# A low-rank tail of two products becomes a sixth chunk of a Strassen step, and the last products run by column slices

## The chip, the cores and the metric

The kernel runs on one core of a Trainium2 chip. Its time is the device time of one execution in microseconds (us). Each kernel is run several times on the same chip as the kernel it is compared with, and medians are compared. One execution is also recorded by the hardware profiler; its trace is what the views below come from.

The engines are called as in the profile: PE (TensorE matmuls; PEld is its weight loads), DVE (VectorE), ACT (ScalarE), POOL (GpSimd) and SP (SyncE, which only issues DMAs here). A name with a q behind it (SPq, ACTq) is an engine's sequencer.

## The reference

Two branches of the same input x (2048 tokens, 640 columns) are mixed by a gate for each token:

```python
a = x @ dft_hid_re.T                        # 640 x 640
b = x @ dft_hid_im.T
A = dft_seq_re @ a - dft_seq_im @ b         # 2048 x 2048 each
q = einsum("nd,dhc->nhc", x, w_q)           # 32 heads, 2 halves of 128
s1, s2 = q1 @ k1.T, q2 @ k2.T               # 16 scores each
...                                         # best 2 of each, best 2 of the 4 sums: 2 of 256 experts
act = gelu(<x, u[e]>);  B = sum over heads and choices of softmax(top)*act * v[e]
g = sigmoid((x * gate_w).sum(-1))
out = g * A + (1 - g) * B
```

## The kernel before

**Precision.** Every large product is made of three fp32r matmuls (`mm3`, lines 126 to 130): an operand is split into a high part, which ACT writes as a copy (line 123), and a low part, which POOL or DVE subtracts (line 124); the three are high × high, high × low and low × high. They show as lines L128, L129 and L130, and almost always have 512 columns.

**The pieces.** The sequence transform comes first, as it is the same work for both hidden matrices: 128 pieces (`seq_piece`; 2 matrices × 4 chunks of 512 tokens × 16 blocks of 128), each of 5 × 3 matmuls into 5 PSUM banks. NPC is their number. A chunk's result is copied out by ACT (L222), multiplied by the gate g on DVE (L193) and stored to DRAM. The other branch runs behind the pieces as a background program: a pump hands out its next step whenever PE has been given enough work. Its last stage builds for every token the weights of the 256 experts: DVE writes two sets of one-hot rows (`hot`, L634), PE multiplies them (L645), ACT masks the product (L604) and DVE sums it (`cd`, L610), after which it goes to DRAM (`gd`). The activations are in DRAM too (`actd`).

**The last part.** What is left is the transform over the hidden dimension, a product with inner length 2 × 640 for each of two halves of the tokens, and the expert branch's z × v, with z = weight × activation × (1 − g), 256 experts (2 rows of 128), and v 256 × 640. The stored chunks a11, a12, a21, a22 (two token chunks by two matrices) and the hidden matrices form a 2 × 2 block product, done by a Strassen form with seven unit products, `UNITS = ("a11", "a12", "s1", "s2", "s4", "s3", "a22")`, for 512 of the 640 columns (two groups of 128 times two). The last 128 columns are a plain product (role W) that rides along in four units. A unit goes over KD = 5 chunks of 128 inner rows; unit and chunk make a step, `step(m)`, 35 for each half (NSTEP), 70 in all. Sums of the token blocks (s1, s2, s3, s4) come from DRAM for the first half and from DVE for the second (`add_a`). Sums of the hidden matrices (`make_sums`, DVE, lines 731 to 735, then `split_sums`) are made among the last pieces.

Operands are split `AHEAD` = 5 steps early into a ring of six (`ring`): two slots of tile WP, four of WS. Raw operands lie in tiles `ra`, handed out by `take` and returned by `give`.

z comes in apart: `load_z` loads g, two rows of activations and two of weights (8 DMAs of 128 × 128); `split_z` makes z on DVE (lines 869 to 873) and splits it into `zo`; v is loaded by `load_v` (L749) at piece NPC − 3 and split at the last part's start (`split_v`); `z_group` adds z × v to the right accumulators at four places of a half.

**The order** is written out by hand: `at(n, f, ...)` has f issued after piece or step n, on whatever engines its instructions name; each engine then works through its instructions in the order of issue. The loads go on SP's queue.

**The end.** In the last unit of the second half the products of the second column group are held back until all others are issued; DVE then subtracts them in two pieces of 256 columns (L994), each followed by its DMA (L995), on SP's and ACT's queue.

Of the kernel before, what the change touches and what calls it, by code (L numbers as in the profile page):

```python
# [16 lines left out]
P = 128  # L17
S = 2048
D = 640
# [17 lines left out]
NSTEP = 7 * KD  # L37
# [54 lines left out]
def gated_mix_kernel(ctx: ExitStack, tc: tile.TileContext, xT, xn, dreT, dimT, wsre, wsim, wq, kT, uT, vv, gw, out):  # L92
# [624 lines left out]
    def t_sum(k, n, a):  # L717

        if n < 2:
            return TS[k][:, (2 * n + a) * 2 * P:][:, :2 * P]  # L720
        if n == 2:
            return TS[5 + k // 2][:, (2 * (k % 2) + a) * 2 * P:][:, :2 * P]
        return DD[:, 0, a, k, 2 * P:4 * P] if n == 3 else TS[k][:, PAIR + a * P:][:, :P]

    def make_sums(k):
        if k == 0:
            T["t"] = big.tile([P, 9 * P], F32, name="tf", tag="xl")
# [3 lines left out]
        nc.vector.tensor_sub(t[:, :4 * P].rearrange("p (n d) -> p n d", n=2), f[:, :, 0:2 * P], f[:, :, 2 * P:4 * P])  # L731
        nc.vector.scalar_tensor_tensor(t3, t1, -1.0, b22, op0=OP.mult, op1=OP.subtract)
        nc.vector.tensor_sub(t5, t1, t5)
        nc.vector.tensor_sub(t6, b22, b12)  # L734
        nc.vector.tensor_sub(t[:, 8 * P:], f[:, 1, 4 * P:], f[:, 0, 4 * P:])  # L735
        bg.credit -= 3.0

    def split_sums(k):
        for n in [k] + ([5 + k // 2] if k % 2 == 0 else []):
            TS[n] = big.tile([P, 2 * D], F32R, name="ts", tag=f"X{(1, 3, 4, 5, 6, 0, 2, 7)[n]}")  # L740
        t = T["t"]
        t1, t5, t3, t6 = (t[:, n * 2 * P:(n + 1) * 2 * P] for n in range(4))
        for n, f in enumerate((t1, t3, t5, t6, t[:, 8 * P:])):
            split(f, t_sum(k, n, 0), t_sum(k, n, 1), nc.gpsimd if n < 2 else nc.vector)
        bg.credit -= 1.0

    def load_v():
        T["f"] = big.tile([P, 2, D], F32, name="dt", tag="xf")
        nc.sync.dma_start(T["f"], vv.rearrange("k p d -> p k d"))  # L749

    def split_v():

        for t in ("xh", "xl"):
            T[t] = big.tile([P, 2, D], F32R, name="v" + t, tag=t)
        split(T["f"], T["xh"], T["xl"], nc.vector)
        for a, t in enumerate(("xh", "xl")):
            nc.scalar.activation(v_neg(a), T[t][:, :, 4 * P:], AF.Copy, scale=-1.0)

    def v_neg(a):
        return TS[5 + a][:, PAIR:].rearrange("p (k d) -> p k d", k=2)  # L760
# [5 lines left out]
    at(NPC - 3, load_v)  # L766
    at(NPC, split_v)
    at(NPC + 28, store_gates, 1)


    fresh, raw_free, raw_tags = deque(), deque(), [("wf", 1)] * 5 + [(f"X{s}", 2) for s in range(10, 16)] + [("xf", 2)]
    raw, sp = {}, {}

    def take(key):
        if not fresh and raw_tags:
            t, n = raw_tags.pop(0)
            if t == "wf":
                fresh.append(big.tile([P, TC], F32, name="ra", tag=t, bufs=5))
            else:
                r = big.tile([P, 2, TC], F32, name="ra", tag=t)  # L780
                fresh.extend(r[:, a] for a in range(2))
        raw[key] = f = (fresh or raw_free).popleft()
        return f
# [51 lines left out]
    def split_step(m):  # L835
        if m < 2 * NSTEP:
            b, (u, k) = m // NSTEP, divmod(m % NSTEP, KD)
            what = UNITS[u]
            key = (b, "s" if b and what in ("s1", "s2", "s4") else what, k)
# [3 lines left out]
            if b == 0 or what in ("a11", "a12", "a22", "s3", "s4"):  # L843
                give(key)

    zop = {}

    def load_z(b, n):
# [5 lines left out]
        for k in range(2):  # L854
            a, f = take((b, "za", k)), take((b, "zf", k))
            nc.sync.dma_start(a, actd[k][:, c * TC:(c + 1) * TC])
            for i in range(4):
                i8 = (4 * c + i) % 8
                nc.sync.dma_start(f[:, i * P:(i + 1) * P],
                                  gd[b][i8 // 4, i8 % 4].rearrange("e f m -> (e f) m")[k * P:(k + 1) * P])  # L860

    def split_z(b, n):

        if not zop:
            for k in range(2):
                zop[k] = big.tile([P, 2, TC], F32R, name="zo", tag=f"X{8 + k}")
        g = raw[b, "g", n]
        s = -1.0 if n == 0 else 1.0
        nc.vector.tensor_scalar(g, g, s, -s, op0=OP.mult, op1=OP.add)
        for k in range(2):  # L870
            a, f = raw[b, "za", k], raw[b, "zf", k]
            nc.vector.tensor_tensor(a, a, f, op=OP.mult)
            nc.vector.tensor_tensor(a, a, g, op=OP.mult)
            split(a, zop[k][:, 0], zop[k][:, 1], nc.gpsimd)
            give((b, "za", k))
            give((b, "zf", k))
        give((b, "g", n))
        bg.credit -= 3.5
# [19 lines left out]
    def post(b, what):  # L898
# [15 lines left out]
        elif what == "q":  # L914
            add("c22", "Y", OP.subtract)
# [5 lines left out]
    def z_group(o, c0, w, first=False, last=False, more=False):  # L921

        for k in range(2):
            h, l = zop[k][:, 0], zop[k][:, 1]
            for d in range(2):
                c = slice((c0 + d) * P, (c0 + d + 1) * P)
                mm3(roles[o][d], T["xh"][:, k, c], T["xl"][:, k, c], h, l, first and k == 0, last and k == 1, more)
                run_bg(0.68)
            if w:
                mm3(roles["W"], w(0)[:, k], w(1)[:, k], h, l, False, last and k == 1)  # L930
                run_bg(0.68)

    held = []

    def step(m):
        b, (u, k) = m // NSTEP, divmod(m % NSTEP, KD)
        what = UNITS[u]
        if k == 0:
# [8 lines left out]
            if what == "a22":  # L947
                z_group("Z", 0, v_neg, first=True)
        split_step(m + AHEAD)
        o, w, w5 = {  # L950
            "a11": ("X", lambda a: DD[:, 0, a, k, 0:2 * P], lambda a: DD[:, 0, a, k, 4 * P:]),
            "a12": ("Z", lambda a: DD[:, 1, a, k, 0:2 * P], lambda a: DD[:, 1, a, k, 4 * P:]),
            "s1": ("Y", lambda a: t_sum(k, 0, a), lambda a: DD[:, 0, a, k, 4 * P:]),
            "s2": ("X", lambda a: t_sum(k, 1, a), None),
            "s4": ("Y", lambda a: DD[:, 1, a, k, 2 * P:4 * P], None),
# [4 lines left out]
        end = k == KD - 1  # L960
        very_last = b == 1 and what == "a22"
        for d in range(1 if very_last else 2):
            c = slice(d * P, (d + 1) * P)
            mm3(roles[o][d], w(0)[:, c], w(1)[:, c], h, l, k == 0 and what in ("a11", "a12", "s1"),
                end and what not in ("a12", "s4"), more)
# [3 lines left out]
        if w5:  # L969
            mm3(roles["W"], w5(0), w5(1), h, l, k == 0 and what in ("a11", "s1"), end and what == "a22")  # L970
# [3 lines left out]
        if what == "a12":  # L974
            z_group("Z", 0, lambda a: T[("xh", "xl")[a]][:, :, 4 * P:], last=True)
        if what == "s4":
            z_group("Y", 2, None, last=True, more=True)
# [4 lines left out]
        if what == "s3":  # L982
            at(NPC + m, post, b, what)
            at(NPC + m, quarter, b)
        elif not very_last:
            at(NPC + m + 1, post, b, what)
        else:
            for d in range(2):
                if d == 1:
                    for n, x in enumerate(held):  # L990
                        mm3(roles["Z"][1], *x, False, n == KD - 1)
                for a in range(d + 1):
                    r = slice(a * TC // 2, (a + 1) * TC // 2) if d else slice(0, TC)
                    nc.vector.tensor_tensor(res["c"][:, d, r], res["c"][:, d, r], roles["Z"][d][:, r], op=OP.subtract)  # L994
                    (nc.scalar if a else nc.sync).dma_start(out[d][:, 3 * TC + r.start:3 * TC + r.stop],  # L995
                                                            res["c"][:, d, r])

    def quarter(b):
        roles["Y"] = [bank(3), bank(4)]
        z_group("Y", 2, None, first=True, last=True)  # L1000
        at(NPC + b * NSTEP + 6 * KD, post, b, "q")

    M = NPC
    for k in range(KD):
        at(M - 6 + k, load_a, 0, "a11", k, 1, 1)
        at(M - 4 + min(k, 3), load_a, 0, "a12", k, 1, 2)
        at(M + k // 2, load_a, 0, "s1", k, 0, 0)
        at(M + 2 + k, load_a, 0, "s2", k, 0, 0)
        at(M + 7 + k, load_a, 0, "s4", k, 0, 0)
        at(M + 12 + k, load_a, 0, "s3", k, 0, 0)  # L1010
        at(M + 18 + k, load_a, 0, "a22", k, 2, 2)
    M = NPC + NSTEP
    for k in range(KD):
        at(M - 8 + k, load_a, 1, "a11", k, 1, 1)
        at(M - 4 + k, load_a, 1, "a12", k, 1, 2)
        at(M + k, load_a, 1, "s", k, 2, 2)
        at(M + k, load_a, 1, "s3", k, 2, 1)
        at(M + 4 + k, add_a, 1, "s", "s3", k, False)
        at(M + 5 + k, load_a, 1, "a11", k, 1, 1)
        at(M + 8 + k, add_a, 1, "s", "a11", k, False)  # L1020
        at(M + 8 + k, add_a, 1, "s3", "a11", k, True)
        at(M + 8 + k, load_a, 1, "a12", k, 1, 2)
        at(M + 13 + k, add_a, 1, "s", "a12", k, True)
        at(M + 21 + k, load_a, 1, "a22", k, 2, 2)
# [79 lines left out]
```

## Time and profile before

| what | us |
|---|---|
| median of the 3 runs | 767.47 (766.01 to 768.31) |
| the profiled execution, its own time | 767.29 |
| its span in the trace | 765.5 |
| last part: from its first matmul to the span's end | 611.74 to 765.5 |
| PE busy, by the page | 759.2 |

The span is what the trace covers; 1.8 us of the profiled execution lie outside. In a row of a timeline the columns are start, duration, engine, line, operation, output and inputs by the program's names, and the number of instructions that were put together (x2), then in brackets the idle time ahead of it and what ended it. Matmul durations overlap, since they are pipelined; what counts is the distance of their starts. In a view of one line or tile the three durations are minimum, median and maximum in ns, with the first and the last start behind them.

### The profile page before, as it was taken

What the parts mean: (1) busy time and instruction counts of PE and PEld (TensorE: products, weight loads), DVE (VectorE), ACT (ScalarE), POOL (GpSimd) and SP (SyncE); (2) the same over time, 40 slices, a digit from 0 to 9 for tenths busy, and PEclk for the clock granted to TensorE, in tenths of its full rate; (3) what the DMA queues carried; (4) which work ended last, traced back from release to release, by engine and by line L of the source; (5) the groups of instructions that cost most, each with busy time, mean ns of one, the idle gap of its engine ahead of it and who ended that gap; (6) DMA issues with size and microseconds to landing.
All of it is one profiled execution on the core that took longest, in us unless ns stands there. A gap on an engine that the chain in (4) does not pass through costs nothing.

```text
span 765.5 us, 11060 instructions
## 1 busy us (share of the span) xinstructions
PE 759.2 (99%) x4085; PEld 620.5 (81%) x4085; DVE 554.9 (72%) x636; ACT 308.5 (40%) x548; POOL 335.1 (44%) x232
## 2 busy tenths in 40 slices
PE   9999999999999999999999999999999999999997
PEld 7777677888888888888888888888888788888886
DVE  6853151589899799999899899579978852437561
ACT  4434123321234432523532774533544653423350
POOL 5533235142242323423158674343456583549270
PEclk9999999999999999999999999999999999999999
DMA  9987996321212322310535352568874696766321
GB/s 336 354 310 187 354 383 204 110 75 42 76 55 75 112 97 62 124 51 21 167 127 167 117 157 73 176 183 272 279 237 166 209 325 212 247 192 196 123 84 69
DMA packets 75654, 130.33 MB, mean 170 GB/s; under 512 B 17104, under 2 KB 24400, under 8 KB 75344
## 3 DMA queue, kind: packets, MB, share of 16 engines
q1 hardware_dynamic: 63424, 113.23, 45.4%
q10 hardware_dynamic: 12176, 16.40, 6.0%
q8 instruction: 32, 0.52, 0.3%
q14 instruction: 22, 0.18, 0.1%
HBM read 102.84 MB, written 25.17 MB: 167 GB/s over the span
## 4 chain that ended last, share of the span: by engine, by line
PE 95%; DVE 2%; DMA 2%; ACT 1%; issue 0%; DVEq 0%
PE b L128 30%; PE b L129 30%; PE b L130 30%; PE b L333 2%; PE b L215 2%; DMA wq<-in_wq 1%; PE b L645 1%; DVE hot L634 1%; DMA wf<-in_wsre 0%; DVE ts L124 0%; DVE cd L610 0%; ACT b L604 0%; ACT ts L123 0%; DVE tf L731 0%; DVE tf L734 0%; DVE tf L735 0%
## 5 line engine op out<-in xcount | busy, mean ns | idle before, releaser
L124 POOL TENSOR_TENSOR WS<-wf,WS 128x512 fp32r<-128x512 f32 x127 | 194.1, 1531 | 257.6 <-ACT WS L123 239.9
L128 PE MATMUL b<-WS,X 128*128 128x512 f32 x620 | 243.4, 393 | 0.0
L129 PE MATMUL b<-WS,X 128*128 128x512 f32 x620 | 241.4, 389 | 0.0
L130 PE MATMUL b<-WS,X 128*128 128x512 f32 x620 | 241.3, 389 | 0.0
L128 PEld LDWEIGHTS b<-WS,X 128*128 128x128 f32 x620 | 116.4, 188 | 28.2 <-issue 3.6
L130 PEld LDWEIGHTS b<-WS,X 128*128 128x128 f32 x620 | 116.4, 188 | 24.3
L129 PEld LDWEIGHTS b<-WS,X 128*128 128x128 f32 x620 | 116.4, 188 | 23.6
L123 ACT ACTIVATE WS<-wf 128x512 fp32r<-128x512 f32 x127 | 79.7, 628 | 110.7 <-PE b L130 62.5
L634 DVE TENSOR_TENSOR hot<-rows,wtab 128x1024 f16<-128x1024 f16 x64 | 60.7, 972 | 15.7 <-PE b L645 15.7
L128 PE MATMUL b<-WU,xh 128*128 128x512 f32 x160 | 62.3, 390 | 0.0
L129 PE MATMUL b<-WU,xh 128*128 128x512 f32 x160 | 62.3, 390 | 0.0
L130 PE MATMUL b<-WU,xl 128*128 128x512 f32 x160 | 62.2, 389 | 0.0
L430 ACT ACTIVATE sc<-b 128x512 f32<-128x512 f32 x32 | 19.8, 618 | 104.6 <-PE b L130 104.6
L124 POOL TENSOR_TENSOR xl<-xf,xh 128x640 fp32r<-128x640 f32 x16 | 26.2, 1643 | 79.8 <-ACT xh L123 79.8
L124 POOL TENSOR_TENSOR WS<-ra,WS 128x512 fp32r<-128x512 f32 x32 | 44.3, 1407 | 27.0 <-ACT WS L123 26.8
L444 DVE TENSOR_REDUCE mm<-sc 128x64 f32<-128x1024 f32 x32 | 38.9, 1217 | 22.6 <-ACT sc L430 22.0
L604 ACT ACTIVATE b<-b,mask 128x128 f32<-128x128 f32 x128 | 43.3, 343 | 19.2 <-PE b L645 16.1
L446 DVE TENSOR_TENSOR eq<-sc,mm 128x1024 f16<-128x1024 f32 x32 | 48.6, 1519 | 1.1
L124 POOL TENSOR_TENSOR WP<-ra,WP 128x512 fp32r<-128x512 f32 x18 | 27.7, 1551 | 29.9 <-ACT WP L123 23.7
L450 DVE TENSOR_REDUCE rr<-eq 128x64 f16<-128x1024 f16 x32 | 39.0, 1220 | 1.1
L193 DVE SCALAR_TENSOR_TENSOR ST<-ST,grow 128x512 f32<-128x512 f32 x40 | 32.2, 863 | 10.1 <-ACT ST L222 10.1
L123 ACT ACTIVATE WS<-ra 128x512 fp32r<-128x512 f32 x46 | 28.3, 629 | 26.4 <-PE b L130 14.0
(155 smaller groups left out, 1217.7 us busy)
## 6 DMA issues: line engine op xcount, KB each, us to landing
wq<-in_wq SPq DMA_DIRECT2D x32, 640.0 KB, 7.6
wf<-in_wsim SPq DMA_DIRECT2D x64, 256.0 KB, 3.6
wf<-in_wsre SPq DMA_DIRECT2D x63, 256.0 KB, 4.7
ra<-pd SPq DMA_DIRECT2D x50, 256.0 KB, 3.8
pd<-ST ACTq DMA_DIRECT2D x35, 256.0 KB, 4.3
xf<-in_xT SPq DMA_DIRECT2D x16, 320.0 KB, 3.4
ra<-pqs SPq DMA_DIRECT2D x20, 256.0 KB, 4.9
xr<-in_xn SPq DMA_DIRECT2D x15, 320.0 KB, 7.2
```

What stands on the lines that cost most here:

```text
L123: nc.scalar.activation(h, f, AF.Copy)
L124: eng.tensor_sub(l, f, h.bitcast(F32))
L128: nc.tensor.matmul(o, wh, ah, start=first, stop=False, skip_group_check=more)
L129: nc.tensor.matmul(o, wh, al, start=False, stop=False, skip_group_check=more)
L130: nc.tensor.matmul(o, wl, ah, start=False, stop=last, skip_group_check=more)
L193: nc.vector.scalar_tensor_tensor(f, f, -1.0 if w else 1.0, g, op0=OP.mult, op1=OP.mult)
L430: nc.scalar.activation(scs[i].rearrange("p h e -> p (h e)")[:, c], ps, AF.Copy)
L444: nc.vector.tensor_reduce(m, sc, op=OP.max, axis=AX.X)
L446: nc.vector.tensor_tensor(eq, sc, m[:, :, None].to_broadcast([P, HH, E]), op=OP.is_equal)
L450: nc.vector.tensor_reduce(r, eq, op=OP.max, axis=AX.X)
L604: nc.scalar.activation(f[:, :, n], f[:, :, n], AF.Copy, scale=mask4[:, n:n + 1])
L634: nc.vector.tensor_tensor(o, a, b, op=op)
```

## The change

Line numbers of the changed kernel are one higher up to line 710 or so (L124 is L125, L869 is L870).

- z and v become a sixth chunk: KZ = 6 chunks and NSTEP = 42 steps a half. v is put in the place of the hidden matrices (`right`), its sums are made as theirs (`make_sums(KD)`), and z's rows in the places of the token blocks; their Strassen sums are made by `sum_z` and `add_a` on DVE. `z_group`, `quarter` and `v_neg` go.
- z's loads move ahead of the operands' (after piece NPC − 6, and −6 before the second half), with the four weight DMAs of a row merged into one; v's load is issued after NPC − 5, its split after NPC − 3, its sums after NPC − 2 and their split at step 3.
- The first z is made after piece NPC − 2, with its four products on POOL; the others on DVE.
- The last held products run as columns 0 to 383, then 384 to 511, each with its subtraction and its DMA.
- The loads of the last part are given new places, and the raw tiles another order.

```diff
-NSTEP = 7 * KD
+KZ = KD + 1
+NSTEP = 7 * KZ
...
+    def right(w, a, k):
+        return T[("xh", "xl")[a]][:, w] if k == KD else DD[:, w, a, k]
...
+        for w in range(2):
+            split(T[KD][:, w], T["xh"][:, w], T["xl"][:, w], nc.vector)
...
-    at(NPC - 3, load_v)
-    at(NPC, split_v)
-    at(NPC + 28, store_gates, 1)
+    at(NPC - 3, split_v)
+    at(NPC - 2, make_sums, KD)
+    at(NPC + 3, split_sums, KD)
+    at(NPC + 14, store_gates, 1)
...
             a, f = take((b, f"a{n + 1}{k + 1}", KD)), take((b, "zf", k))
             nc.sync.dma_start(a, actd[k][:, c * TC:(c + 1) * TC])
-            for i in range(4):
-                ...
+            nc.sync.dma_start(f.rearrange("p (t m) -> p t m", t=4),
+                              gd[b][n].rearrange("t e f m -> (e f) t m")[k * P:(k + 1) * P])
...
+    def make_z(b, n):
+        eng = nc.vector if b or n else nc.gpsimd
         g = raw[b, "g", n]
+        nc.vector.tensor_scalar(g, g, -1.0, 1.0, op0=OP.mult, op1=OP.add)
         for k in range(2):
+            a, f = raw[b, f"a{n + 1}{k + 1}", KD], raw[b, "zf", k]
+            eng.tensor_tensor(a, a, f, op=OP.mult)
+            eng.tensor_tensor(a, a, g, op=OP.mult)
...
+    def sum_z(b):
+        s, a21 = take((b, "s", KD)), raw.pop((b, "a21", KD))
+        nc.vector.tensor_add(s, a21, raw[b, "a22", KD])
+        nc.vector.tensor_add(a21, a21, raw[b, "a11", KD])
+        raw[b, "s3", KD] = a21
...
-            for d in range(2):
+            for d, r, eng in ((0, slice(0, TC), nc.sync), (1, slice(0, 3 * P), nc.scalar), (1, slice(3 * P, TC), nc.sync)):
                 if d == 1:
-                    for n, x in enumerate(held):
-                        mm3(roles["Z"][1], *x, False, n == KD - 1)
-                for a in range(d + 1):
-                    ...
+                    for n, (wh, wl, h, l) in enumerate(held):
+                        mm3(roles["Z"][1][:, r], wh, wl, h[:, r], l[:, r], n == 0, n == KD)
+                nc.vector.tensor_tensor(res["c"][:, d, r], res["c"][:, d, r], roles["Z"][d][:, r], op=OP.subtract)
+                eng.dma_start(out[d][:, 3 * TC + r.start:3 * TC + r.stop], res["c"][:, d, r])
...
+    at(M - 6, load_z, 0, 0)
     for k in range(KD):
-        at(M - 6 + k, load_a, 0, "a11", k, 1, 1)
-        at(M - 4 + min(k, 3), load_a, 0, "a12", k, 1, 2)
+        at(M - 5 + k // 2, load_a, 0, "a11", k, 1, 1)
+    at(M - 5, load_v)
...
-        for n, i in ((0, -1), (1, 21)):
-            at(M + i, load_z, b, n)
-            at(M + i + 4, split_z, b, n)
+        at(M + 1, load_z, b, 1)
+        for n, i in ((0, -1 if b else -2), (1, 6)):
+            at(M + i, make_z, b, n)
+        at(M + 9, sum_z, b)
```

POOL's row at the end of the pieces and the start of the last part, before (the WP and WS rows are the low parts of the operands of steps 0, 1, 2, 3, 4 and 5):

```order
L124 TENSOR_TENSOR WP_5275<-ra_5213,WP_5275 128x512
L124 TENSOR_TENSOR WP_5275<-ra_5244,WP_5275 128x512
L124 TENSOR_TENSOR WS_88<-ra_5273,WS_88 128x512
L124 TENSOR_TENSOR WS_88<-ra_5299,WS_88 128x512
L124 TENSOR_TENSOR WS_88<-ra_5365,WS_88 128x512
L124 TENSOR_TENSOR WS_88<-ra_5271,WS_88 128x512
```

The same place of the changed kernel:

```order
L125 TENSOR_TENSOR WP_5285<-ra_5251,WP_5285 128x512
L125 TENSOR_TENSOR WP_5285<-ra_5253,WP_5285 128x512
L873 TENSOR_TENSOR ra_5213<-ra_5213,ra_5215 128x512
L874 TENSOR_TENSOR ra_5213<-ra_5213 128x512
L873 TENSOR_TENSOR ra_5218<-ra_5218,ra_5219 128x512
L874 TENSOR_TENSOR ra_5218<-ra_5218,ra_5213 128x512
L125 TENSOR_TENSOR WS_88<-ra_5253,WS_88 128x512
L125 TENSOR_TENSOR WS_88<-ra_5283,WS_88 128x512
```

The four products of the first z (L873 activation × weight, L874 times 1 − g) now stand between the low parts of steps 1 and 2.

DVE's row at that place before, where `cd` are the experts' last sums and ST the five gate products of the last chunk:

```order
L610 TENSOR_REDUCE cd_4293<-b6_5309 128x8x16
L610 TENSOR_REDUCE cd_4293<-b7_5326 128x8x16
L193 SCALAR_TENSOR_TENSOR ST_68<-ST_68,grow_5362 128x512 x5
L124 TENSOR_TENSOR vxl_5429<-dt_5295,vxh_5428 128x1280
L869 TENSOR_SCALAR ra_5390<-ra_5390 128x512
```

And of the changed kernel:

```order
L125 TENSOR_TENSOR vxl_5306<-dt_5255,vxh_5305 128x640 x2
L611 TENSOR_REDUCE cd_4293<-b6_5322 128x8x16
L611 TENSOR_REDUCE cd_4293<-b7_5339 128x8x16
L736 TENSOR_TENSOR tf_5377<-dt_5255 128x512
L737 SCALAR_TENSOR_TENSOR tf_5377<-tf_5377,dt_5255 128x256
L738 TENSOR_TENSOR tf_5377<-tf_5377 128x256
L739 TENSOR_TENSOR tf_5377<-dt_5255 128x256
L740 TENSOR_TENSOR tf_5377<-dt_5255 128x128
L870 TENSOR_SCALAR ra_5213<-ra_5213 128x512
L194 SCALAR_TENSOR_TENSOR ST_68<-ST_68,grow_5375 128x512 x5
```

v's low parts, its five sums and the factor 1 − g (L870) now stand ahead of the gate products; the first two of v's low parts also ahead of the last `cd` sums.

PE's row at the end, of the changed kernel, where the products of 384 columns pass into those of 128 in the same PSUM tile b6 (before, all fifteen are 128x512 in a row):

```order
L129 MATMUL b6_6377<-WS_88,ts_5240 128x384
L130 MATMUL b6_6377<-WS_88,ts_5240 128x384
L131 MATMUL b6_6377<-WS_88,ts_5240 128x384
L129 MATMUL b6_6377<-WP_5285,ts_4934 128x128 [waits DVE_49]
L130 MATMUL b6_6377<-WP_5285,ts_4934 128x128
L131 MATMUL b6_6377<-WP_5285,ts_4934 128x128
```

The wait in the fourth row is for the subtraction of the 384 columns.

More of the change, by code (lines that the diff above doesn't have):

```diff
@@ L836, in split_step @@
         if m < 2 * NSTEP:
-            b, (u, k) = m // NSTEP, divmod(m % NSTEP, KD)
+            b, (u, k) = m // NSTEP, divmod(m % NSTEP, KZ)
             what = UNITS[u]
-            key = (b, "s" if b and what in ("s1", "s2", "s4") else what, k)
+            key = (b, "s" if (b or k == KD) and what in ("s1", "s2", "s4") else what, k)
             sp[m] = ring(m)[:, 0], ring(m)[:, 1]
@@ L919, in post @@
             put(b, 1, 0, res["c"])
-    def z_group(o, c0, w, first=False, last=False, more=False):
-        for k in range(2):
-            h, l = zop[k][:, 0], zop[k][:, 1]
-            for d in range(2):
[L926 to L931, printed above, removed]
     held = []
     def step(m):
-        b, (u, k) = m // NSTEP, divmod(m % NSTEP, KD)
+        b, (u, k) = m // NSTEP, divmod(m % NSTEP, KZ)
         what = UNITS[u]
@@ L959, in step @@
         more = what in ("s2", "s3", "s4")
-        end = k == KD - 1
+        end = k == KD
         very_last = b == 1 and what == "a22"
@@ L963, in step @@
             c = slice(d * P, (d + 1) * P)
-            mm3(roles[o][d], w(0)[:, c], w(1)[:, c], h, l, k == 0 and what in ("a11", "a12", "s1"),
-                end and what not in ("a12", "s4"), more)
+            mm3(roles[o][d], w(0)[:, c], w(1)[:, c], h, l, k == 0 and what in ("a11", "a12", "s1", "a22"), end, more)
             run_bg(0.68)
@@ L969, in step @@
         if w5:
-            mm3(roles["W"], w5(0), w5(1), h, l, k == 0 and what in ("a11", "s1"), end and what == "a22")
+            mm3(roles["W"], w5(0), w5(1), h, l, k == 0 and what in ("a11", "s1"),
+                end and what in ("a12", "a22"))
             run_bg(0.68)
@@ L987, in step @@
         else:
[L988 removed]
+            for d, r, eng in ((0, slice(0, TC), nc.sync), (1, slice(0, 3 * P), nc.scalar), (1, slice(3 * P, TC), nc.sync)):
                 if d == 1:
[L990 to L1001 removed]
+                    for n, (wh, wl, h, l) in enumerate(held):
+                        mm3(roles["Z"][1][:, r], wh, wl, h[:, r], l[:, r], n == 0, n == KD)
+                nc.vector.tensor_tensor(res["c"][:, d, r], res["c"][:, d, r], roles["Z"][d][:, r], op=OP.subtract)
+                eng.dma_start(out[d][:, 3 * TC + r.start:3 * TC + r.stop], res["c"][:, d, r])
     M = NPC
+    at(M - 6, load_z, 0, 0)
     for k in range(KD):
[L1005 to L1011 removed]
+        at(M - 5 + k // 2, load_a, 0, "a11", k, 1, 1)
+    at(M - 5, load_v)
+    for k in range(KD):
+        at(M - 3 + (0, 1, 2, 2, 3)[k], load_a, 0, "a12", k, 1, 2)
+        at(M + 2 + k // 2, load_a, 0, "s1", k, 0, 0)
+        at(M + 5 + k, load_a, 0, "s2", k, 0, 0)
+        at(M + 11 + k, load_a, 0, "s4", k, 0, 0)
+        at(M + 17 + k, load_a, 0, "s3", k, 0, 0)
+        at(M + 24 + k, load_a, 0, "a22", k, 2, 2)
     M = NPC + NSTEP
+    at(M - 6, load_z, 1, 0)
     for k in range(KD):
```

91 lines of the change are left out of this document (36 added, 55 removed).

## The prediction

> **What bounds the kernel.** I read the page's head first, then the waits of TensorE (PE), then the timelines of all engines around the two ends of the last part, since the change touches nothing earlier than some pieces before it.
>
> ```profile
> span 765.5 us, 11060 instructions
> ...
> PE 759.2 (99%) x4085; PEld 620.5 (81%) x4085; DVE 554.9 (72%) x636; ACT 308.5 (40%) x548; POOL 335.1 (44%) x232
> ...
> PE b L333 <- DMA wq<-in_wq: 0.8, 1, 0.8
> PE b L283 <- PEq L1096: 0.8, 1, 0.8
> PE b L645 <- DVE hot L634: 0.5, 1, 0.5
> PE b L215 <- ACT WS L253: 0.3, 1, 0.3
> ```
>
> PE is busy for 99% of the span, and all its waits together are 2.4 us, of which only the third, 0.5 us, lies near the last part. So a matmul taken out is worth its spacing in time, as long as whatever feeds the others keeps up; and every wait that the change creates on PE is paid in full. The spacing and the tail behind the last matmul come from the timeline of the last part:
>
> ```profile
> 611.74 0.39 PE L128 MATMUL b<-WP,DD 128*128 128x512 f32 x1
> ...
> 757.94 0.39 PE L128 MATMUL b<-WS,ts 128*128 128x512 f32 x1
> ...
> 761.12 0.39 PE L130 MATMUL b<-WS,ts 128*128 128x512 f32 x1
> 761.54 0.75 DVE L994 TENSOR_TENSOR ST<-ST,b 128x256 f32<-128x256 f32 x2 [3.39 <-PE b L130]
> 762.33 0.35 ACTq L995 DMA_DIRECT2D out_y<-ST  x1
> ```
>
> 611.74 is the first matmul of the last part and 757.94 the first of the fifteen held back for the last 128 columns; between them lie 645. (757.94 − 611.74) / 645 = 0.2267 us from start to start, with no gap. Behind the last matmul follow two subtractions by VectorE (DVE), the last DMA's issue at 762.33, and 765.5 − 762.33 = 3.17 us until the span's end.
>
> The sum below is made against this profiled execution: 767.29 us, 1.8 of it outside the span. The median of the runs shown is 767.47, so 0.18 is added at the end. About 0.3%, 2.3 us, is what a measurement of this kernel can tell from no change.
>
> **The matmuls.** Before, z costs 60 matmuls for each half: 2 rows of 128 experts times 10 products times 3. As a sixth chunk it costs 7 units × 2 × 3 plus 4 × 3 for the fifth column group, 54. For both halves that is 12 fewer; the held ones rise from 15 to 18, so ahead of the tail it is 630 instead of 645. 15 × 0.2267 = **−3.40 us** there; the three more held ones are in the tail's price.
>
> **The tail.** Before, from the first held matmul to the span's end: 765.5 − 757.94 = 7.56 us. After, 18 products of 384 columns, a DVE subtraction of them, and 18 of 128 columns, the first of which waits for that subtraction because both write into one PSUM bank; then a subtraction of 128 columns and a 64 KB DMA. The narrowest product of this kind in the trace has 256 columns:
>
> ```profile
> 148.59 0.28 PE L128 MATMUL b<-xh,WU 128*128 128x256 f32 x1
> ...
> 152.06 0.28 PE L130 MATMUL b<-xh,WU 128*128 128x256 f32 x1
> L128 PEld LDWEIGHTS b<-xh,WU 128*128 128x128 f32 x10 | 1.9, 192 | 0.0
> ```
>
> The first and the last of thirty lie 3.47 us apart, 0.120 each. So 384 columns take about (0.2267 + 0.120) / 2 = 0.173, and 17 × 0.173 = 2.95 us pass to the eighteenth's start. From a start to DVE's start were 761.54 − 761.12 = 0.42 us; 0.05 less for the narrower product. The subtraction of 384 columns takes some 0.55, between 0.75 for two of 256 and the 0.68 that its 512-wide kin take below. With 0.2 for the signal PE resumes 2.95 + 0.37 + 0.55 + 0.2 = 4.07 us after the first held matmul. Then come 17 spacings of 128-column products, 0.26 to DVE's start, 0.28 for its 128 columns, 0.05 to the issue and 3.1 for the last DMA: 7.76 us without the 17 spacings.
>
> What a 128-column product costs no row shows. The straight line through 512 and 256 columns gives 0.067, so 17 take 1.1 and the tail is 8.9, +1.3. If it costs as much as a 512-column one, 0.227, they take 3.9, the tail is 11.6 and the price **+4.1**. The nearest row is the 256-column one, 0.120; each product loads its own weights, in 0.192 us by the last row above, and one such load for each product would not get shorter with the columns. I take 0.120: 17 × 0.120 = 2.04, tail 9.8, **+2.2**. The Trainium skill, "TensorE: Matmul & The Clock Gate", section "Back-to-back issue gap", gives about 81 ns for N = 128 in streams with weight loads, which would make the tail 0.7 us shorter than I take; no run so far has such a row.
>
> **The start of the last part.** The change moves v's load, its split, the sums of v and the first z here.
>
> ```profile
> L749 SPq DMA_DIRECT2D dt<-in_vv x1: 396/396/396, 599.2 to 599.2; - x1
> DMA to landing us min/median/max: 4.0/4.0/4.0
> ...
> 601.31 1.14 ACT L123 ACTIVATE WP<-ra 128x512 fp32r<-128x512 f32 x2
> 605.35 2.85 ACT L604 ACTIVATE b<-b,mask 128x128 f32<-128x128 f32 x8 [2.90 <-PE b L645]
> 602.01 3.18 POOL L124 TENSOR_TENSOR WP<-ra,WP 128x512 fp32r<-128x512 f32 x2 [0.21 <-ACT WP L123]
> 603.97 1.77 DVE L634 TENSOR_TENSOR hot<-hot,rows 128x1024 f16<-128x1024 f16 x1
> 605.79 0.44 PE L645 MATMUL b<-hot 128*64 128x64 f16 x16 [0.48 <-DVE hot L634]
> 608.23 0.69 DVE L610 TENSOR_REDUCE cd<-b 128x128 f32<-128x512 f32 x1 [0.69 <-ACT b L604]
> 608.82 1.29 POOL L124 TENSOR_TENSOR WS<-ra,WS 128x512 fp32r<-128x512 f32 x1 [3.63 <-ACT WS L123]
> 616.05 0.39 PE L129 MATMUL b<-WS,DD 128*128 128x512 f32 x1
> ```
>
> v lands at 599.2 + 4.0 = 603.2 and will do so after too: the sums of the fifth chunk on DVE gate its issue in both. ScalarE (ACT) now splits v between the two WP operands, in its idle stretch up to 605.35. A 512-column split takes 1.14 / 2 = 0.57, v's 1280 columns some 1.4, so the high part of the second WP operand is made by 605.2 instead of 602.45; its low part by GpSimd (POOL) then ends near 606.5, ahead of its use in the last part. The eight masks at 605.35 stay, as they are gated by PE. POOL now rests while DVE's operation at 603.97 runs, which should end about a microsecond sooner, so that the wait of 0.48 at 605.79 goes: −0.45.
>
> From there DVE's row is longer: two low parts of v in its idle stretch, the two column sums up to 608.92 (gated by the masks), then five sums of v, then the factor 1 − g, and only then the five gate products (L193). POOL's row has four products of the first z ahead of the low part of step 2's operand, which it made at 608.82 before; the second of the four needs 1 − g. Their prices:
>
> ```profile
> L731 DVE TENSOR_TENSOR tf<-dt x5: 675/682/1186, 565.1 to 595.5; 128x512 f32<-128x512 f32 x5
> L732 DVE SCALAR_TENSOR_TENSOR tf<-tf,dt x5: 426/1322/1333, 565.8 to 596.8; 128x256 f32<-128x256 f32 x5
> L734 DVE TENSOR_TENSOR tf<-dt x5: 412/958/1541, 566.5 to 597.5; 128x256 f32<-128x256 f32 x5
> L735 DVE TENSOR_TENSOR tf<-dt x5: 277/280/828, 568.0 to 598.3; 128x128 f32<-128x128 f32 x5
> L869 DVE TENSOR_SCALAR ra<-ra x4: 418/422/1522, 617.0 to 735.0; 128x512 f32<-128x512 f32 x4
> L872 DVE TENSOR_TENSOR ra<-ra x8: 678/684/1780, 618.4 to 737.6; 128x512 f32<-128x512 f32 x8
> L124 POOL TENSOR_TENSOR WS<-ra,WS x32: 1289/1303/2571, 608.8 to 745.2; 128x512 fp32r<-128x512 f32 x32
> L124 POOL TENSOR_TENSOR zo<-ra,zo x8: 1285/1688/1739, 623.0 to 740.2; 128x512 fp32r<-128x512 f32 x8
> ```
>
> By the minima, since POOL stands still meanwhile, DVE needs 0.675 + 0.426 + 0.412 + 0.412 + 0.277 = 2.2 us for the sums (the third at the fourth's price) and 0.42 for the factor: 608.92 + 2.6, less the overlap of neighbours, is about 611.3. Then POOL has three products and the low part before PE can go on: 4 × 1.29 = 5.2 us alone, to 616.5; or 4 × 1.6 to 1.7, as z's low parts cost when DVE works on two operands beside them, to about 617.7. DVE does run its five gate products just then. PE takes that low part with the second matmul of step 2, before at 616.05. The start therefore costs +0.45 to +1.7 with the gain at 605.79 given back in the wait. I take the row nearest in kind, z's: **+1.6**. Below, −0.45, if 1 − g comes early enough to hide it all. Above, +2.8: if v lands a microsecond later, ACT's queue (second WP operand, masks, then everything behind) waits for it, and DVE and POOL shift with it.
>
> The SBUF page speaks against this more strongly. The Trainium skill, "SBUF — State Buffer", section "SBUF: two separate sides", says that DVE with two SBUF inputs and GpSimd lock each other out for a whole instruction; by it POOL and DVE would alternate, which is the fourth case below. The median of 1.69 against 1.29 alone shows less than that, the maxima of 1.78 and 2.57 show it at times.
>
> **What else moves, at nothing.** The first z's loads go ahead of the operands on SP's queue, four in one, and are there when POOL reads them. Over the last part DVE gains four operations net, ACT six splits (0.6 each), POOL two splits and the four products.
>
> ```profile
> 687.00:700.00 13.00, 13.00 (x59) 10.78 (x58) 10.45 (x9) 6.79 (x12) 11.40 (x8) 1.00 0.67 204
> 713.00:726.00 13.00, 13.00 (x59) 10.74 (x59) 10.92 (x18) 5.52 (x10) 3.08 (x1) 1.00 0.41 132
> ```
>
> In these two stretches (busy time of PE, PEld, DVE, ACT, POOL in 13 us) DVE, third, is fullest, and still has 2.1 to 2.5 us free while PE never waits. The changed order spreads the sums of z over steps 9 to 21. If that cover is gone, a late operand costs about one DVE operation, 0.7 us, or one of POOL's, 1.3.
>
> **Sum.** −3.40 + 2.2 + 1.6 = +0.4: 767.7 against the profiled execution, **767.9** on the median.
>
> **Rivals.**
> (1) *The narrow products cost as much as wide ones* and the tail takes 11.6 us. For it: no product under 256 columns is in the trace, and the weight loads don't shrink. Against: halving from 512 to 256 halved the spacing nearly in full. It decides from 0.17 us each; at 0.227 the time is 767.9 + 1.9 = 769.8, and with a bad start it is slower beyond the bound.
> (2) *The cuts win.* The start is hidden and the narrow products follow the straight line: −3.40 − 0.45 + 1.3 = −2.55, 764.9 on the median. For it: POOL idles long before 608.82, so the products might find their place. Against: the factor 1 − g stands last in DVE's row behind operations that PE's masks gate.
> (3) *v comes late*: +1.2 on the start, 769.1. For it: 603.2 + 1.4 + 0.57 leaves 0.2 us to ACT's masks at 605.35, so any lateness beyond that is passed on; against: this load took 4.0 us under the same traffic.
> (4) *POOL and DVE alternate strictly*: 611.3 + 4 × (1.29 + 0.68) = 619.2, 3.15 late instead of 1.6, 769.4. For: the maxima above; against: the medians.
> (5) *The removal isn't real*, because another step waits that I hold covered: one to three late operands of 1.3, 769 to 772.
>
> **Chances.** Forecast 0.42, (1) 0.30, (2) 0.11, (3) 0.05, (4) 0.05, (5) 0.07. The forecast's case spans about 766.5 to 769. Half of (1), whose start can be dear or cheap, half of (4), a fifth of (3) and most of (5) end over 769.8, as does 0.05 of the forecast's: 0.28 slower. Faster needs less than 765.2: most of (2), 0.10. The rest, 0.62, is within 0.3%. The range reaches from 765.2, which cuts off (2), to 771.0, which is (1) with v late.
>
> **What would show it.** The matmuls of the last part keep 0.2267 us and their count falls by 15. The rows of 128 columns show their spacing directly, and the span from the first 384-column product to the end is 9.8 (8.9, 11.6). PE's waits would list a new one on POOL's low part at the second matmul of step 2, of 0.5 to 1.7 us, and lose the one on `hot`. POOL's second product would start right behind DVE's 1 − g near 611.3. The forecast is wrong if PE's waits have another entry of over a microsecond, or none, or if the tail is outside 8.9 to 11.6.

## The result and the profile after

| kernel | runs | median us | lowest to highest |
|---|---|---|---|
| before | 22 | 767.08 | 766.01 to 768.31 |
| changed | 22 | 768.43 | 766.83 to 770.93 |

The ratio is 1.0019, with a 95% interval of 1.0012 to 1.0026: 0.9 to 2.0 us slower, 1.35 us by the medians. That is inside the predicted range and inside the 0.3% that the prediction called the same. The profiled execution of the changed kernel, 766.83 us with a span of 765.0, happens to be the fastest of its 22. So its parts are read here, but not its total.

First the page's head line and the waits of PE after:

```profile
span 765.0 us, 11081 instructions
...
PE b L130 <- POOL WS L125: 2.5, 1, 2.5
PE b L284 <- PEq L1080: 0.8, 1, 0.8
PE b L129 <- DVE ST L977: 0.6, 1, 0.6
```

The wait on `hot` is gone, and two new ones are there: on POOL's low part, 2.5 us, and on the subtraction in the tail, 0.6 us. Before's waits for `wq` and at L215, 1.1 us in the first hundred, aren't in this execution; nothing was changed there, and they come and go.

The start of the last part, from the timelines of PE, DVE and POOL:

```profile
603.66 0.69 PE L646 MATMUL b<-hot 128*64 128x64 f16 x32
...
609.86 0.39 PE L129 MATMUL b<-WP,DD 128*128 128x512 f32 x1
...
613.94 0.39 PE L129 MATMUL b<-WS,DD 128*128 128x512 f32 x1
616.84 0.50 PE L130 MATMUL b<-WS,DD 128*128 128x512 f32 x1 [2.51 <-POOL WS L125]
...
609.56 0.42 DVE L870 TENSOR_SCALAR ra<-ra 128x512 f32<-128x512 f32 x1
609.89 7.44 DVE L194 SCALAR_TENSOR_TENSOR ST<-ST,grow 128x512 f32<-128x512 f32 x5
...
606.03 1.28 POOL L873 TENSOR_TENSOR ra<-ra 128x512 f32<-128x512 f32 x1
610.12 1.61 POOL L874 TENSOR_TENSOR ra<-ra 128x512 f32<-128x512 f32 x1 [2.81 <-DVE ra L870]
611.69 1.74 POOL L873 TENSOR_TENSOR ra<-ra 128x512 f32<-128x512 f32 x1
613.52 1.60 POOL L874 TENSOR_TENSOR ra<-ra 128x512 f32<-128x512 f32 x1
615.07 1.71 POOL L125 TENSOR_TENSOR WS<-ra,WS 128x512 fp32r<-128x512 f32 x1
```

POOL's first product is done at 607.3. It then stands for 2.81 us until DVE has made 1 − g (L870), which stands behind v's sums. The other three and the low part of step 2 in the last row take 6.66 us, to 616.78. PE would have taken the second matmul of step 2 at 613.94 + 0.23 = 614.17 and took it at 616.84, 2.67 late. The first row holds the experts' products, of which before sixteen were issued at 604.87 and sixteen behind the wait on `hot`; now all 32 go in one run. DVE's gate products (L194), on two operands of SBUF, took two and a half times as long beside POOL:

```profile
L193 DVE SCALAR_TENSOR_TENSOR ST<-ST,grow x5: 678/693/807, 609.9 to 612.6; 128x512 f32<-128x512 f32 x5
...
L194 DVE SCALAR_TENSOR_TENSOR ST<-ST,grow x5: 681/1760/1783, 609.9 to 615.6; 128x512 f32<-128x512 f32 x5
```

The first row is before, the second after: a median of 1.76 us instead of 0.69.

The tail after, from the timelines of PE and DVE:

```profile
755.49 0.33 PE L129 MATMUL b<-WP,ts 128*128 128x384 f32 x1
...
758.46 0.34 PE L131 MATMUL b<-WS,ts 128*128 128x384 f32 x1
758.84 0.56 DVE L977 TENSOR_TENSOR ST<-ST,b 128x384 f32<-128x384 f32 x1 [3.14 <-PE b L131]
759.45 0.33 PE L129 MATMUL b<-WP,ts 128*128 128x128 f32 x1 [0.65 <-DVE ST L977]
759.61 0.28 PE L130 MATMUL b<-WP,ts 128*128 128x128 f32 x1
...
761.40 0.28 PE L131 MATMUL b<-WS,ts 128*128 128x128 f32 x1
```

The eighteen products of 384 columns start 2.97 / 17 = 0.175 us apart. From 759.61 to 761.40 lie 16 spacings, 0.112 us each: a quarter of the columns takes half the time of a 512-column product. From the first held product to the span's end it is 765.0 − 755.49 = 9.51 us, against 7.56 before.

### The profile page after: what moved, and what is told of

Same layout as the page of the kernel before. It is cut to its first block, busy times and chain, and to the rows that moved or that the text cites. A ratio compares the mean times of both kernels' runs of the same rounds, so it can differ in the third digit from the quotient of the medians.

```text
span 765.0 us, 11081 instructions
## 1 busy us (share of the span) xinstructions
PE 757.7 (99%) x4091; PEld 619.7 (81%) x4091; DVE 568.2 (74%) x649; ACT 314.4 (41%) x558; POOL 345.4 (45%) x240
## 4 chain that ended last, share of the span: by engine, by line
PE 97%; POOL 1%; DVE 0%; DMA 0%; ACT 0%; issue 0%; POOLq 0%
PE b L129 31%; PE b L130 30%; PE b L131 30%; PE b L334 2%; PE b L216 2%; PE b L646 1%; DMA wf<-in_wsre 0%; ACT b L605 0%; POOL ra L874 0%; POOL WS L125 0%; POOL ra L873 0%; DVE ST L977 0%; DVE cd L611 0%; ACT WS L254 0%; DVE tf L736 0%
## 5 line engine op out<-in xcount | busy, mean ns | idle before, releaser
L125 POOL TENSOR_TENSOR WS<-wf,WS 128x512 fp32r<-128x512 f32 x127 | 193.8, 1528 | 256.3 <-ACT WS L124 245.1
L124 ACT ACTIVATE WS<-wf 128x512 fp32r<-128x512 f32 x127 | 79.7, 628 | 109.6 <-PE b L131 59.9
L635 DVE TENSOR_TENSOR hot<-rows,wtab 128x1024 f16<-128x1024 f16 x64 | 62.4, 999 | 15.5 <-PE b L646 15.5
L125 POOL TENSOR_TENSOR xl<-xf,xh 128x640 fp32r<-128x640 f32 x16 | 25.9, 1621 | 80.4 <-ACT xh L124 75.9
L125 POOL TENSOR_TENSOR WS<-ra,WS 128x512 fp32r<-128x512 f32 x39 | 55.1, 1428 | 8.8 <-ACT WS L124 8.5
L124 ACT ACTIVATE WS<-ra 128x512 fp32r<-128x512 f32 x55 | 34.6, 631 | 54.1 <-PE b L131 38.9
L125 POOL TENSOR_TENSOR WP<-ra,WP 128x512 fp32r<-128x512 f32 x18 | 27.6, 1543 | 44.4 <-ACT WP L124 44.4
L194 DVE SCALAR_TENSOR_TENSOR ST<-ST,grow 128x512 f32<-128x512 f32 x40 | 36.2, 967 | 9.2 <-ACT ST L223 9.2
```

Of the source, the lines that this page charges most:

```text
L124: nc.scalar.activation(h, f, AF.Copy)
L125: eng.tensor_sub(l, f, h.bitcast(F32))
L194: nc.vector.scalar_tensor_tensor(f, f, -1.0 if w else 1.0, g, op0=OP.mult, op1=OP.mult)
L635: nc.vector.tensor_tensor(o, a, b, op=op)
```

## The experiments

They were timed in three groups, each on one chip with runs of the kernel before, whose medians were 766.53, 767.16 and 767.03. So ratios are compared between groups, and medians inside one.

### The factor 1 − g early (first group)

```diff
     at(NPC - 3, split_v)
+    at(NPC - 3, flip_first)     # DVE: 1 - g of the first z, from make_z
```

> The changed kernel, but the factor 1 - g of the first z is made on DVE right after v's low parts, ahead of the last column sums and the sums of v. Theory (POOL's z products wait for 1 - g, and that wait puts step 2's low part late): POOL's second product starts near 607.3 instead of 610.12, the four end by 611.2 to 612.8 and step 2's low part by 614.2, so the wait of 2.5 us on PE goes or is under 0.5, and the time falls by 2 to 2.5 us from the changed kernel's 768.4, to about 766. Rival (POOL is too slow for four products and a low part anyhow while DVE runs its five gate products): the wait stays over 1 us and the time falls by less than 1.

Measured: 765.65, ratio 0.9990 (0.9981 to 0.9998). From the changed kernel's 1.0019 that is 0.0029, 2.2 us, as the theory has it. POOL and DVE, and the one wait of PE in the last part's first half:

```profile
608.23 1.30 POOL L880 TENSOR_TENSOR ra<-ra 128x512 f32<-128x512 f32 x1 [0.43 <-DVE ra L774]
...
612.62 5.92 POOL L125 TENSOR_TENSOR WS<-ra,WS 128x512 fp32r<-128x512 f32 x4
...
611.43 1.52 DVE L738 TENSOR_TENSOR tf<-tf 128x256 f32<-128x256 f32 x1
...
637.10 0.50 PE L129 MATMUL b<-WP,DD 128*128 128x512 f32 x1 [0.36 <-ACT ST L972]
```

The low parts begin at 612.62 instead of 615.07, and the wait of 2.5 us is gone. Now v's sums on DVE lie beside POOL's products, and one of them takes 1.5 us instead of 0.42 (L738); the gate products behind them begin at 615.60 instead of 609.89. A wait of 0.36 comes later, which the last experiment ties to this; by the distance of the matmuls' starts, PE loses 0.8 us there.

### The wide tail (first group)

```diff
-            for d, r, eng in ((0, slice(0, TC), ...), (1, slice(0, 3 * P), ...), (1, slice(3 * P, TC), ...)):
+            for d in range(2):        # as before: 18 products of 512, then two subtractions of 256
```

> The changed kernel, but its eighteen held products run with 512 columns, as before, and the subtraction and DMA follow in two pieces of 256. Theory (the column slices cost in the tail: a wait of 0.65 us for the subtraction in between, and narrow products that take 0.11 each): first held product to the span's end 7.56 + 3 x 0.2267 = 8.24 us instead of 9.51, so 1.3 us faster than the changed kernel. Rival (the smaller last subtraction and DMA pay for the slices): no faster, or slower.

Measured: 765.89, ratio 0.9998 (0.9989 to 1.0007), 1.6 us under the changed kernel's ratio. In its trace the tail takes 765.9 − 757.33 = 8.57 us, 0.94 less than with the slices and 0.33 more than the 8.24 expected. The ratio gives more, but its interval reaches down to 0.9. The profiled execution, 767.66, was the longest of the eleven, and shows why (first the tail's first product; then the windows, with the granted clock third from the end; then PE's timeline):

```profile
757.33 0.39 PE L129 MATMUL b<-WP,ts 128*128 128x512 f32 x1
...
617.00:618.00 1.00, 0.81 (x2) 0.71 (x3) 0.69 (x1) 0.00 (x0) 1.00 (x2) 0.50 0.56 217
618.00:619.00 1.00, 1.00 (x3) 0.78 (x3) 0.00 (x0) 0.00 (x0) 1.00 (x2) 0.50 0.45 174
619.00:620.00 1.00, 1.00 (x4) 0.74 (x3) 0.00 (x0) 0.00 (x0) 1.00 (x1) 0.50 0.92 219
620.00:621.00 1.00, 1.00 (x5) 0.81 (x4) 0.00 (x0) 0.15 (x1) 1.00 (x2) 0.81 0.83 102
...
617.19 0.79 PE L130 MATMUL b<-WS,DD 128*128 128x512 f32 x1 [2.51 <-POOL WS L125]
617.78 0.63 PE L131 MATMUL b<-WS,DD 128*128 128x512 f32 x1
618.21 0.63 PE L129 MATMUL b<-WS,DD 128*128 128x512 f32 x1
```

Behind the same wait of 2.51 us the clock stands at 0.50 from 617.0 to about 620.4 (the mean of 0.81 in the last row is 0.38 us at half speed), some 3.4 us, and products start 0.43 us apart instead of 0.227. PE works in the last 3.2 us of it, at half speed, so this costs 1.6 us on top of the wait. Three of the eleven executions had a mean clock of 0.996 to 0.997; they took 767.5 in the mean, the other eight, at 0.999, 765.9.

### The first z on DVE (first group)

```diff
-        eng = nc.vector if b or n else nc.gpsimd
+        eng = nc.vector
```

> The changed kernel, but all four products of the first z on DVE, behind 1 - g, as the other z have them. Theory (it is the place in POOL's queue that holds step 2's low part): POOL makes that low part right behind the second WP one, near 607.5, PE doesn't wait, DVE's five gate products shift by 4 x 0.68 = 2.7 us but run at 0.69 each without POOL's products beside them, and the time falls by 2 to 2.5 us, as in the run with the early factor. Rival (DVE is the bound of that stretch): another wait on PE for a DVE product or for z appears, of a microsecond or more, and the time stays.

Measured: 766.31, ratio 1.0000 (0.9991 to 1.0009): 1.5 us under the changed kernel, less than expected. The wait at step 2 went, but two others came. The rival had expected another wait, though of a microsecond or more and for a DVE product or z:

```profile
616.62 6.32 DVE L194 SCALAR_TENSOR_TENSOR ST<-ST,grow 128x512 f32<-128x512 f32 x4
...
635.59 0.50 PE L130 MATMUL b<-WP,ts 128*128 128x512 f32 x1 [0.85 <-POOL WP L125]
637.43 0.51 PE L129 MATMUL b<-WP,DD 128*128 128x512 f32 x1 [0.41 <-ACT ST L966]
```

The gate products begin at 616.62 instead of 609.89 and still take 1.6 us each, now beside POOL's low parts. The expectation that they would run at 0.69 was wrong: from 611.12 on POOL makes low parts without a gap. The two waits cost more than the 0.85 and 0.41 that are listed: by the starts of the products around them PE loses 2.0 us. The 2.8 us of the first wait and the 0.7 of clock that the sections below find, less these 2.0, make the 1.5 measured. One of the eleven executions, 768.46, had a mean clock of 0.996; no trace shows why.

### Both mends (first group)

> Both the early factor and the 512-wide held products. If the two losses are separate, the gains add: 2.0 to 2.5 and 1.3, so about 764.5 to 765, which is 2.2 to 2.6 us (0.3%) under the kernel before. If the time of the changed kernel is lost elsewhere in most executions (its median lies 1.6 us over its profiled execution), the gain is smaller than that and the kernel is no faster than before.

Measured: 764.49, ratio 0.9977 (0.9967 to 0.9988). On this chip that is 1.16 us under the early factor alone: its tail is 8.52 us instead of 9.51. The two losses are separate and add, as expected.

### The changed kernel again (second group)

> The changed kernel as it is, beside the other kernels of this group. If a part of its time is the TensorE clock, which in the run with the wide tail stood at 0.50 for 3.6 us behind the wait of 2.5 us, then its executions fall in two groups, those of a mean clock of 0.995 to 0.997 about 1.8 us over those of 0.998 and 0.999. Rival (the spread has another source): no such groups, and the time doesn't go with the clock.

Measured: 768.52, ratio 1.0022 (1.0012 to 1.0031). Six of eleven executions had a mean clock of 0.996 or 0.997 and took 769.65 in the mean; the other five took 767.86. In the 22 of the result it was 7 at 769.79 and 15 at 767.98. Both differences are 1.8 us, near the 1.6 worked out above (the 3.6 us in the expectation were read from whole windows). The edges of the groups overlap, as other things vary by a microsecond too. Of the kernel before, none of the 66 executions in the three groups was below 0.999. The six runs with the factor early, above and below, have 51 executions, none below 0.998.

What the mean clock can tell has a limit. Neither profiled execution of the changed kernel, both at 0.998, has a low clock behind the wait; both have one behind the last matmul, where it costs nothing:

```profile
761.00:762.00 1.00, 0.67 (x7) 0.53 (x5) 0.29 (x1) 0.00 (x0) 0.00 (x0) 1.00 0.00 0
762.00:763.00 1.00, 0.00 (x0) 0.00 (x0) 0.00 (x0) 0.00 (x0) 0.00 (x0) 0.53 0.06 20
```

In this kernel the 3.3 us behind the last matmul take 0.0022 off the mean at most, which shows as 0.998, so 0.997 and less means a low clock while PE had work. Some 3.4 us at half speed behind the wait alone would show as 0.998 too, so some of the others may have had it.

### A longer stall (second group)

```diff
             eng.tensor_tensor(a, a, g, op=OP.mult)
+            if k and not b and not n:
+                eng.tensor_tensor(f, f, g, op=OP.mult)     # on POOL, result unused
```

> The run with the wide tail, and one more product on POOL ahead of step 2's low part (its result isn't used): the wait on PE grows from 2.5 to about 4.1 us. Theory (TensorE's clock halves for some 3.6 us when PE has stood still long enough, and 2.5 us reach it only in some executions): nearly all executions now have a mean clock of 0.997 or less, and the median is 1.6 + 1.8 = 3.4 us over that of the wide tail's undisturbed ones, 769 on that chip. Rival (the low clock comes by chance): 1.6 us more, with the low clock as rare as before.

```profile
PE b L130 <- POOL WS L125: 4.2, 1, 4.2
```

Measured: 770.79, ratio 1.0044 (1.0031 to 1.0058), 3.5 us over the wide tail's 0.9998, as the theory says. All five executions had a mean clock of 0.997 or 0.995. In the trace PE goes on at 620.12, and the clock is at 0.50 from about 620.8 to 624.2. The wait grew by 1.7 us and the low clock went from 3 in 11, or 6 in 11 of the changed kernel on this chip, to 5 in 5; without the first wait it was 0 in 51. So the clock follows the wait and isn't chance.

### A bank of its own for the last 128 columns (second group)

```diff
+                o = bank(3) if r.start else roles["Z"][d]
...
-                        mm3(roles["Z"][1][:, r], wh, wl, h[:, r], l[:, r], n == 0, n == KD)
+                        mm3(o[:, r], wh, wl, h[:, r], l[:, r], n == 0, n == KD)
```

> The run with the early factor, but the last 128 columns go to a PSUM bank of their own, so that PE need not wait for the subtraction of the 384. Theory (of the 1.3 us that the slices cost, 0.65 are that wait and the rest the eighteen narrow products at 0.11 instead of a quarter of 0.227): 0.6 us less than the early factor alone, 0.6 more than both mends. Rival (the last subtraction and DMA set the end): no change.

```profile
756.59 0.33 PE L129 MATMUL b<-WP,ts 128*128 128x384 f32 x1
...
759.73 0.22 PE L129 MATMUL b<-WP,ts 128*128 128x128 f32 x1
```

Measured: 765.68, ratio 0.9979 (0.9970 to 0.9988), against 0.9990 for the early factor alone on another chip; the intervals overlap, so the time alone doesn't settle it. The trace does: PE goes on at 759.73, 0.17 after the last product of 384 columns, without a wait, and the tail takes 765.2 − 756.59 = 8.61 us. The wait is nearly all that the slices cost, 0.90 of the 0.94 us, where 0.6 of 1.3 was expected; with it gone they are level with the wide tail's 8.52 and 8.57.

### The gate products ahead of v's sums (second and third group)

```diff
-    at(NPC - 2, make_sums, KD)
+    at(NPC + 1, make_sums, KD)
```

> The run with both mends, but v's sums are issued three steps later, behind the five gate products of the last chunk. Theory (the 0.4 us that PE still waits for ACT at 636.6 come from the gate products, which are stored late, hold the loads of s1 on SP's queue, and so ACT's splits): the products end near 616 instead of 623, the stores go 5 us earlier, the wait goes, and the time is 764.1 against 764.5 on that chip, 0.4 less. Rival (ACT is late by itself): the wait stays and the time is the same.

Measured: 764.04, ratio 0.9962 (0.9950 to 0.9975), 0.0015 or 1.15 us under both mends alone, more than a wait of 0.39. So it was run beside its counterpart on one chip:

> Both mends (early factor, 512-wide held products) once more, beside the next kernel on one chip, since the two were timed on different chips before (0.9977 and 0.9962 of the kernel before, whose intervals overlap). If the late stores of the gate products cost only the one wait of 0.39 us in the trace, this one stands 0.4 us over the next; if the larger distance of the two ratios is real, 1.1 us.

> Both mends and v's sums behind the gate products, beside the one before: 0.4 us less by the wait at the second unit's first products, 1.1 less by the ratios; the same time would mean that the wait isn't what separates them. Against the kernel before: 0.996 to 0.998.

Measured: 765.71 for both mends, ratio 0.9982 (0.9973 to 0.9991), and 763.98 with the gate products first, ratio 0.9962 (0.9949 to 0.9974). First the rows of the former, then of the latter:

```profile
616.69 8.58 DVE L194 SCALAR_TENSOR_TENSOR ST<-ST,grow 128x512 f32<-128x512 f32 x5
618.49 7.13 SPq L204 DMA_DIRECT2D pd<-ST  x5
628.19 9.93 SPq L803 DMA_DIRECT2D ra<-pqs  x13
636.09 0.39 PE L129 MATMUL b<-WP,ts 128*128 128x512 f32 x1
637.22 0.50 PE L130 MATMUL b<-WP,ts 128*128 128x512 f32 x1 [0.74 <-POOL WP L125]
637.55 0.39 PE L131 MATMUL b<-WP,ts 128*128 128x512 f32 x1
638.25 0.39 PE L131 MATMUL b<-WP,ts 128*128 128x512 f32 x1
639.05 0.50 PE L129 MATMUL b<-WP,DD 128*128 128x512 f32 x1 [0.42 <-ACT ST L972]
639.39 0.39 PE L130 MATMUL b<-WP,DD 128*128 128x512 f32 x1
...
609.47 7.63 DVE L194 SCALAR_TENSOR_TENSOR ST<-ST,grow 128x512 f32<-128x512 f32 x5 [0.86 <-DMA grow<-gdr]
610.34 7.12 SPq L204 DMA_DIRECT2D pd<-ST  x5
620.02 11.75 SPq L803 DMA_DIRECT2D ra<-pqs  x13
```

The chain is in them: the gate products late, their five stores late on SP's queue, the loads of s1 (`pqs`) behind those, and so the low parts and the copy of the second unit. In this execution PE waits twice, 1.16 us by the list of waits; in the other order, not at all. By the starts it loses more: from 636.09 to 637.55 and from 638.25 to 639.39 it starts four products in 2.60 us, which take 4 × 0.227 = 0.91 elsewhere. That is 1.69, near the 1.7 by the medians. (The loads of `wq` in the first hundred microseconds, 0.8 us longer in the one execution than in the other, lie outside this count.) In the earlier trace of both mends the same count gives 1.03 around the listed wait of 0.39, against 1.15 by the ratios. So the 0.4 expected by the wait was too low, as it counted the wait by its listed idle time; the 1.1 by the ratios was nearer. This version beats both kernels: 0.38% under the one before.

## Why the prediction held, and where its terms were off

**Matmuls.** 630 products from 609.86 to 755.49 less 2.67 of the wait and 0.1 behind it: 142.86 / 630 = 0.2268. The −3.40 stands.

**The tail.** 9.51 − 7.56 = +1.95 where +2.2 was taken. The handover from DVE to PE, 0.2 in the sum, was 0.05 (from 758.84 + 0.56 to 759.45). The narrow product, 0.112, lies by its nearest row, 0.120; rival (1), 0.227, is out. The Trainium skill's 81 ns ("TensorE: Matmul & The Clock Gate", section "Back-to-back issue gap") lies below it: the measurement decides. The wait was seen by its cause and at its size. Not seen was that it is nearly all that the slices cost, and that another bank takes it away.

**The start.** Place, releaser and mechanism were right: the second matmul of step 2, POOL's low part behind three products that wait for 1 − g. The size was low. From the first of the experts' products to that matmul it was 616.05 − 604.87 = 11.18 us before and is 616.84 − 603.66 = 13.18 now: +2.0 instead of +1.6. Shifted by the 1.21 us that these products come earlier, 1 − g was due at 610.1 and is done at 609.98, as reckoned. The step that was off is the four POOL operations: 6.66 us, where the row of z's low parts was read as 1.6 to 1.7 each and the low end, 6.4, went into the sum. By that row's median, 1.69, it would have been +2.0. The listed wait, 2.51, lies outside the 0.5 to 1.7 that was said, for another reason: with the wait on `hot` gone, PE comes to this matmul 2.67 − 2.0 = 0.67 earlier, and the wait was reckoned against its old time. The sum isn't touched by that, as the gain was given back in it.

Of rival (4), DVE's side is seen: 1.76 us instead of 0.69. POOL's operations took 1.6 to 1.74, not the 1.97 of a strict turn, so the rival's +3.15 was too much. The rule of the Trainium skill that stands beside it ("SBUF — State Buffer", section "SBUF: two separate sides"), a lock for a whole instruction, is borne out only so far.

**The term that was missing.** "Every wait that the change creates on PE is paid in full": it is paid more than in full. In 13 of 33 executions of the changed kernel the mean clock was 0.997 or less, and these took 1.8 us more by their means, +0.7 over all. That the clock falls behind this wait is seen in the traces of the wide tail and of the longer stall; of the changed kernel no such execution was traced. The Trainium skill has the gate ("TensorE: Matmul & The Clock Gate", section "What's actually happening"): half speed after an idle window of about 3.4 us, whose start is free-running. The trace agrees on the half speed and on the 3.4 us that it lasts; but a wait of 2.5 us was enough at times. Nor does the length of a wait alone decide: the clock fell 2.3 us into the wait in the wide tail's trace and 0.6 us behind its end in the longer stall's, and in the trace of the kernel before it stays at 1.00 for the 4.0 us from the last matmul's end to the span's.

**What was held at nothing.** In the stretch from 687 to 700 the fullest of the engines that feed PE is POOL, 11.40 of 13 us, not DVE with 10.45; 1.6 us were free there, not over 2. It did no harm: PE waits for no operand in that part of the changed kernel. Rival (5) had a covered step wait; none did in the changed kernel. With the first wait mended, one or two came at the second unit and cost 0.8 to 2.0 us by the starts.

**The sum.** −3.40 + 1.95 + 2.0 + 0.7 = +1.25, against 1.35 by the medians and 0.9 to 2.0 by the ratio. The predicted +0.4 lies below that interval, 0.4 of it by the start and 0.7 by the clock, with 0.25 back from the tail. So the forecast of no clear change held, but half of the change that there was comes from a term that it did not have; the range covered it by its width.

## What to carry to other kernels

An operation that is handed to an idle engine stands in that engine's queue ahead of what was there, and waits for the slowest of its inputs: here one factor of 0.42 us, placed last in another engine's row, held up the operand behind four products and made TensorE 2.67 us late. On a kernel bound by TensorE, look for the longest wait first: one of 2.5 us here cost the clock as well in some executions. Count what a wait costs by the starts of the matmuls around it: 1.16 us of listed idle time were 1.69 here. And when a wait is mended, read the next one in the trace: here it was a chain of late products, stores and loads some twenty microseconds on.

## What the runs showed of the hardware

- With a PE wait of 2.5 us in the trace, the mean clock was 0.997 or less in 16 of 44 executions (the changed kernel and the one with the wide tail); with one of 4.2 us in all 5; with that wait mended in none of 51. Where traces show it, the clock stood at half speed for 3.4 us. One of the 11 executions with the first z on DVE had 0.996 as well, for a reason that isn't known.
- A wait costs more than its listed idle time, as the products next to it start late too: 1.16 us were 1.69, and 2.51 were 2.67 and 0.1 behind it.
- fp32r products with a weight load each start 0.227 us apart at 512 columns, 0.175 at 384, 0.120 at 256 and 0.112 at 128: below 256 there was little left to gain.
- Operations of DVE on two operands in SBUF took 1.76 instead of 0.69 us while POOL worked, and POOL's took 1.6 to 1.74 instead of 1.29.
